# Loads, a conversion and the sums of output weights placed at other steps of a fused attention, MoE, MoE kernel

## The chip, the cores and the metric

The kernel runs on one NeuronCore of a Trainium2 chip. The metric is the device time of one execution in microseconds. Before the change three runs gave 1335.27, 1335.88 and 1336.69 us, median 1335.88. A verdict against this time is read from the runs of both kernels on the same chip.

## What is computed

The reference chains three blocks on 4608 tokens (8 batches of 576), in float32:

```python
scores = scale * q_c @ k_c.T            # chunks of 64 tokens, 8 heads of 64
attn = softmax(scores); x = attn @ v_c  # [4608, 512]
h = x @ w_in                            # [4608, 1024]
solu = h * softmax(h)
ln = (solu - mu) / sqrt(var + 1e-6) * g_ln
y = ln @ w_out                          # [4608, 512]
g = y @ w_gate; val = y @ w_val         # [4608, 1536] each
out = (g * sigmoid(g) * val) @ w_out2   # [4608, 512]
```

All weights arrive as float64 and are converted on the chip. Each float32 product is made of three passes over a high and a low part (PASSES, hi*hi, hi*lo, lo*hi).

## The kernel before

**Stages.** In the profiled execution attention and the first MoE matrix run to about 316 us, the matrix that gives y to about 518 us, the two matrices w_gate and w_val to about 1054 us, and w_out2 from there to the end. The change touches the third of these and the few units where the fourth begins.

**The third stage** (the double loop over s and n, L1012 to L1053). Tokens go in NSG = 5 segments of widths 512, 384, 512, 384, 512 (each width is half of a segment's tokens); for each segment there are FT = 12 steps, one per block of 128 hidden columns. The global step number is G = n + 12 s; `late` counts the steps of the last segment from 0 (G = 48). A step (`step`, L887) is a 2x2 block product with 7 sub-products instead of 8. Each sub-product (`product`, L863) is 6 matmuls into one of the PSUM tiles psA to psD, in the order A, C, B, D, A, C, D: products 4, 5 and 6 add to A, C and D, so each starts only when the earlier content of its bank has been read. ScalarE reads product 0 into p1 (L897) and product 1 into p5 (L899); VectorE makes p1 (L902), u3 (L904), the gate (L908), c12 in p5's buffer (L911), p1 again (L914) and three products (L915 to L917); GpSimd adds p5 to u3 (L905). So c12 can be written only when GpSimd's L905 has read p5, and the next step's L897 can write p1 only when L916 has read it.

**Work placed beside the steps**, written out by hand in program order, which is also each queue's order:

- `y_load(s + 1)` (L748) fetches the next segment's y from DRAM into `rawy` (a view of `ry`), 4 quarters (b11, b12, b21, b22) of one or two DMAs each, all on SyncE's queue; `y_units` (L759) is a list of 22 small units that turn it into the 7 operands: 8 GpSimd subtractions (L771) and 14 splits, each a ScalarE copy (L774) and a VectorE subtraction (L775). They are handed out a few per step; the last of them belong to the last step of the segment.
- The conversion of w_out2 in 24 pieces: `v_load` (L934, a DMA into a raw buffer), two steps on `v_mag` (ScalarE L79 and L85, GpSimd L92), after that step `v_bits` (VectorE L98 and L106, GpSimd L127), one step on `v_store` (L948, a DMA to `wo_dram`). Pieces alternate between two magnitude buffers `vms` and go round three raw buffers `vraws`, all inside the tile `mix`. LOADS lists the steps that load. v_mag of piece u overwrites the buffer that v_store of piece u - 2 read.
- In the last segment the converted rows come back as pairs p = 0 to 5: `t_load` (L925, 2 DMAs), `t_sums` (L954, 4 GpSimd subtractions of 128x256), `t_split` (L959, a ScalarE copy L965 and a VectorE subtraction L966 of 128x1792). The raw rows lie in the two halves of `ry`; t_split(p) for p < 3 issues t_load(p + 2) at its end. The sums of p are queued on GpSimd ahead of a step's L905.
- From `late` = 6 on `x_load`, `x_sums` (L985, 4 VectorE operations, L993), `x_high` (ScalarE L999) and `x_low` (VectorE L1004) prepare the operands of the last stage.
- SyncE's queue further carries the u stores (L885), the weight loads `w_load` (L742, ring of three) and all of the above, in order: an entry that waits holds all behind it.

**The fourth stage** runs units (n, i) of 7 sub-products with 3 passes (L1089, per unit 6 matmuls for each of pa, pb, pc and 3 for pd); `prepare(n)` puts x_high(n + 2), x_sums(n + 3), x_low(n + 2) ahead of unit n; every 6 units `evac` (L1096) empties the banks through ScalarE, VectorE (L1100) and GpSimd.

Of the kernel before, what the change touches and what calls it, by code (L numbers as in the profile page):

```python
# [23 lines left out]
def attn_moe_moe2_kernel(  # L24
# [681 lines left out]
    with ExitStack() as ph2:  # L706
# [40 lines left out]

        def y_load(s):  # L748
            for i, (half, k) in enumerate(((0, 0), (1, 0), (0, 2), (1, 2))):
                t, n = FIRST[s] + half * WIDTHS[s], 0  # L750
                while n < WIDTHS[s]:
                    m, o = divmod(t + n, TOK)
                    c = min(TOK - o, WIDTHS[s] - n)
                    nc.sync.dma_start(
                        out=rawy[:, :, i, n:n + c], in_=y_dram[m][:, k:k + 2, o:o + c]
                    )
                    n += c
# [65 lines left out]
        for m in range(1, NG):  # L823
            for d in range(KD):
# [8 lines left out]
                if last_m and d == 0:  # L833
                    stage_.close()
                    p2.close()
                    cp = ph2.enter_context(pool("cp"))
                    mix = cp.tile([P, 7 * HC], I64, tag="mix", name="mix")
                    flat = mix.bitcast(F32)
                    tt = flat[:, 0:6 * HC].rearrange("p (a n) -> p a n", a=3)
                    vms = [flat[:, i * HC:(i + 1) * HC] for i in (6, 7)]  # L840
                    vraws = [mix[:, i * HC:(i + 1) * HC] for i in (4, 5, 6)]
                    for i in range(2):
                        osb = cp.tile([P, TOK], F32, tag="osb", name="osb", bufs=2)
                    yk[1] = yk_tile(1)
                    w_load()
                    ka_ = ExitStack()
                    ka = ka_.enter_context(pool("ka"))
                    ahead_y = y_units(0)
# [72 lines left out]

        halves = list(ry.rearrange("p (j a n) -> j p a n", j=2, a=8))
        tw, tx = {}, {}

        def t_load(p):  # L925
            x = tx[p] = halves[p % 2 if p < 5 else 2]
            for j, dst in enumerate((x[:, 1:8:6], x[:, 2:7:4])):
                nc.sync.dma_start(
                    out=dst, in_=wo_dram[2 * p + j].rearrange("p (b n) -> p b n", b=2)
                )  # L930
# [8 lines left out]
        def v_mag(u):  # L939
            vc[u] = conv_a(None, vw.pop(u), vms[u % 2])  # L940
            conv_r(vc[u])
# [11 lines left out]

        def t_sums(p):  # L954
            t4, b11, b21, t1, t2, t3, b22, b12 = (tx[p][:, i] for i in range(8))
            for o, a, b in ((t1, b12, b11), (t2, b22, t1), (t3, b22, b12), (t4, b21, t2)):
                nc.gpsimd.tensor_tensor(out=o, in0=a, in1=b, op=ALU.subtract)

        def t_split(p):  # L959
            if p == 0:  # L960
                t = cb.tile([P, NS, 2, HC], F32R, tag="tw", name="tw")
            else:
                t = t_home[p]
# [4 lines left out]
            )  # L968
            if p < 3:
                t_load(p + 2)  # L970

# [6 lines left out]
        def x_load(n):  # L978
            if n >= NU:
                return  # L980
            x = xs[n] = halves[1 - n % 2 if n < 4 or n % 4 > 1 else 3 + n % 2]
            nc.sync.dma_start(out=x[:, 2:4], in_=unit_src(n, 0))
# [27 lines left out]
        todo = []  # L1010
        LOADS = (*range(1, FT + 1), *range(2 * FT - 2, 3 * FT - 2))
        for s in range(NSG):  # L1012
            for n in range(FT):
# [3 lines left out]
                if s + 1 < NSG:  # L1017
                    if n == (s == 0):
                        y_load(s + 1)
                    if n == (3 if s == 0 else 1):  # L1020
                        todo = y_units(s + 1)
                if late == 0:
                    t = cp.tile([P, 3, NS, 2, HC], F32R, tag="ykb", name="tw")
                    t_home = {i + 1: t[:, i] for i in range(3)}
                    t_home[4] = cp.tile([P, NS, 2, HC], F32R, tag="mix", name="tw")
                    t_load(0)
                    t_load(1)
                if 1 <= late < 6:
                    t_sums(late - 1)
                if late in (6, 8):  # L1030
                    x_load(late // 2 - 3)
                if G - 3 in LOADS:
                    v_store(LOADS.index(G - 3))
                if mag is not None:
                    v_mag(mag)
                step(s, n)
                if mag is not None:
                    v_bits(mag)
                if G in LOADS:
                    v_load(LOADS.index(G))  # L1040
                k = -(-len(todo) // (FT - n)) if todo else 0
                for x in todo[:k]:
                    x()
                todo = todo[k:]
                if 2 <= late < 7:
                    t_split(late - 2)
                if late in (7, 9):
                    x_sums(late // 2 - 3)
                if late in (9, 10):
                    x_high(late - 9)  # L1050
                    x_low(late - 9)
                if late == 11:
                    x_sums(2)  # L1053
        u_store()
# [10 lines left out]
        x_low(2)  # L1065
        t_sums(5)
        x_sums(3)

        def prepare(n):
            if n:  # L1070
                x_high(n + 2)
                x_sums(n + 3)
                x_low(n + 2)
            if n == 2:
                t_split(5)
# [97 lines left out]
```

## Time and profile before

| what | before |
|---|---|
| median of 3 runs | 1335.88 us (1335.27 to 1336.69) |
| the profiled execution's own time | 1336.44 us |
| its span, first to last instruction | 1334.7 us |
| TensorE matmul busy | 1299.1 us, 97% |
| VectorE, ScalarE, GpSimd busy | 962.8, 612.8, 434.5 us |
| mean granted TensorE clock | 0.994 of full speed |
| DMA queue of SyncE, share of 16 engines | 66.2% |

Times are in us from the start of the span. PE is TensorE's matmuls, PEld its weight loads, DVE VectorE, ACT ScalarE, POOL GpSimd, SPq the queue of SyncE that issues DMAs. An entry in brackets is the idle time of the engine before the instruction and what ended it. Matmuls overlap, so the listed duration of six is longer than the distance from one group's start to the next.

### The profile page before, as it was taken

The page shows a single profiled execution, that of the slowest core. Times are in us where ns is not written, and L with a number is a line of the kernel's source. Part 1 is how long each engine was busy: PE and PEld are TensorE (multiplying, and loading weights), DVE is VectorE, ACT ScalarE, POOL GpSimd, SP SyncE. Part 2 cuts the span into 40 slices and gives each one's busy share as a digit, 9 for nine tenths or more (in the row PEclk, how much of TensorE's full clock was granted, in tenths as well). Part 3 has the DMA queues.
Part 4 walks back from the last instruction along what each step waited for, and adds up shares of the span by engine and source line. Part 5 has one row for each costly group of instructions (what it writes and reads, how often), then busy time and mean ns, then how long its engine had stood idle before and what let it go on. Part 6 is the DMA issues. An engine that isn't in the chain of part 4 may idle for free.

```text
span 1334.7 us, 24970 instructions
## 1 busy us (share of the span) xinstructions
PE 1299.1 (97%) x9554; PEld 1182.0 (89%) x9554; DVE 962.8 (72%) x1564; ACT 612.8 (46%) x962; POOL 434.5 (33%) x581
## 2 busy tenths in 40 slices
PE   4999999999999999999899999999989999999998
PEld 3788888888999999888899888999868899999998
DVE  7788888885577765576566666766557898877875
ACT  5566666666566654334233333333223343333331
POOL 5455555554343342243322333231331200000010
PEclk9999999999999999999899999999989999999999
DMA  7355566665799997877989877988767444444341
GB/s 253 119 175 175 179 184 183 185 220 164 274 392 352 370 353 279 309 300 281 339 301 322 320 302 279 362 312 312 280 230 261 142 142 142 132 139 141 129 150 57
DMA packets 149063, 318.31 MB, mean 238 GB/s; under 512 B 11216, under 2 KB 98256, under 8 KB 141264
## 3 DMA queue, kind: packets, MB, share of 16 engines
q1 hardware_dynamic: 142608, 308.06, 66.2%
q10 hardware_dynamic: 6336, 8.65, 1.8%
q8 instruction: 75, 1.23, 0.4%
q14 instruction: 44, 0.36, 0.1%
HBM read 225.45 MB, written 91.23 MB: 237 GB/s over the span
## 4 chain that ended last, share of the span: by engine, by line
PE 90%; DVE 5%; DMA 2%; POOL 1%; issue 1%; ACT 1%; SPq 0%; POOLq 0%; DVEq 0%; ACTq 0%
PE y L166 15%; PE h L378 15%; PE pa L870 10%; PE pd L870 10%; PE pc L870 10%; PE opc L1089 5%; PE pb L870 5%; PE opa L1089 5%; PE opb L1089 5%; PE so_ps L262 3%; PE tr L459 3%; PE opd L1089 2%; PE pt L332 1%; DMA ry<-wo 1%; DVE hl L1004 1%
## 5 line engine op out<-in xcount | busy, mean ns | idle before, releaser
L378 PE MATMUL h<-wA,x 128*128 128x512 f32 x864 | 216.7, 399 | 0.6 <-ACT x L358 0.3
L166 PE MATMUL y<-lnT,wB 128*128 128x384 f32 x1152 | 200.7, 334 | 0.6 <-ACT ysb L172 0.6
L166 PEld LDWEIGHTS y<-lnT,wB 128*128 128x128 f32 x1152 | 199.5, 188 | 0.9 <-ACT ysb L172 0.9
L378 PEld LDWEIGHTS h<-wA,x 128*128 128x128 f32 x864 | 156.8, 188 | 32.1 <-ACT x L358 1.5
L905 POOL TENSOR_TENSOR u<-u,p 128x512 f32<-128x512 f32 (+1 forms) x60 | 70.7, 1179 | 218.0 <-DVE u L904 208.6
L870 PE MATMUL pa<-yka,ws 128*128 128x512 f32 x432 | 112.5, 397 | 6.1 <-ACT p L897 6.1
L907 ACT ACTIVATE u<-pa 128x512 f32<-128x512 f32 (+1 forms) x60 | 33.3, 556 | 175.4 <-PE pa L870 175.4
L870 PE MATMUL pc<-yka,ws 128*128 128x512 f32 x432 | 110.5, 391 | 0.0
L870 PE MATMUL pd<-yka,ws 128*128 128x512 f32 x432 | 109.8, 389 | 0.2 <-DVE u L904 0.2
L870 PEld LDWEIGHTS pa<-yka,ws 128*128 128x128 f32 x432 | 82.2, 191 | 24.3 <-ACT p L897 7.4
L1100 POOL TENSOR_TENSOR o<-o,p 128x256 f32<-128x256 f32 x35 | 25.8, 746 | 238.5 <-DVE o L1100 238.5
L870 PEld LDWEIGHTS pc<-yka,ws 128*128 128x128 f32 x432 | 82.0, 190 | 17.3
L1089 PE MATMUL opc<-tw,hl 128*128 128x256 f32 x648 | 96.2, 284 | 0.6 <-DVE o L1100 0.6
L870 PEld LDWEIGHTS pd<-yka,ws 128*128 128x128 f32 x432 | 81.0, 188 | 17.4 <-DVE u L904 0.6
L1089 PE MATMUL opb<-tw,hl 128*128 128x256 f32 x648 | 95.4, 283 | 0.3 <-DVE o L1100 0.3
L1089 PE MATMUL opa<-tw,hl 128*128 128x256 f32 x648 | 95.5, 283 | 0.0
L1089 PEld LDWEIGHTS opc<-tw,hl 128*128 128x128 f32 x648 | 85.4, 192 | 1.6 <-DVE o L1100 1.0
L1089 PEld LDWEIGHTS opb<-tw,hl 128*128 128x128 f32 x648 | 85.5, 192 | 0.5 <-DVE o L1100 0.5
L1089 PEld LDWEIGHTS opa<-tw,hl 128*128 128x128 f32 x648 | 85.6, 192 | 0.2
L908 DVE TENSOR_TENSOR u<-pa,u 128x512 f32<-128x512 f32 (+1 forms) x60 | 38.3, 638 | 65.0 <-ACT u L907 64.9
L999 ACT ACTIVATE hl<-ry 128x1792 fp32r<-128x1792 f32 x28 | 47.7, 1705 | 80.3 <-PE opd L1089 33.2
L912 ACT ACTIVATE u<-p 128x512 f32<-128x512 f32 (+1 forms) x60 | 35.4, 590 | 105.9 <-DVE p L911 105.9
(131 smaller groups left out, 2657.7 us busy)
## 6 DMA issues: line engine op xcount, KB each, us to landing
ws<-ws SPq DMA_DIRECT2D x60, 1792.0 KB, 7.7
ln<-lt SPq DMA_DIRECT2D x72, 256.0 KB, 3.0
lr<-ln SPq DMA_DIRECT2D x24, 768.0 KB, 7.1
u<-u SPq DMA_DIRECT2D x36, 512.0 KB, 5.4
ry<-u SPq DMA_DIRECT2D x56, 256.0 KB, 3.3
work<-u SPq DMA_DIRECT2D x52, 256.0 KB, 3.3
ws<-shi SPq DMA_DIRECT2D x12, 896.0 KB, 9.3
qt<-in_q SPq DMA_DIRECT2D x36, 256.0 KB, 3.6
```

The source lines that it names most:

```text
L166: nc.tensor.matmul(ys[u], lhsT=wB[:, f, a, d * P:(d + 1) * P], rhs=lnT[m][:, b, f, :], start=(n == 0), stop=(n == NY - 1),)
L262: nc.tensor.matmul(out[b * CH:(b + 1) * CH, c, n], lhsT=lhsT[r, h], rhs=rhs[r, h], start=True, stop=True, tile_position=(c * CH, b * CH),)
L378: nc.tensor.matmul(h[:, n * DM:(n + 1) * DM], lhsT=x[:, a, k, :], rhs=wA[:, n * KD + k, b, :], start=(j == 0), stop=(j == NH // 2 - 1),)
L459: nc.tensor.transpose(tr[:, f, :], so[:, c0:c0 + P], ident)
L870: nc.tensor.matmul(ps, lhsT=w[:, a, kk * P:(kk + 1) * P], rhs=y[:, b, kk], start=(first and n == 0), stop=(n == 5), skip_group_check=True,)
L905: nc.gpsimd.tensor_tensor(out=u3, in0=u3, in1=p5, op=ALU.add)
L907: nc.scalar.activation(out=sa, in_=psA, func=AF.Sigmoid)
L908: nc.vector.tensor_tensor(out=sa, in0=psA, in1=sa, op=ALU.mult)
L912: nc.scalar.activation(out=sb, in_=c12, func=AF.Sigmoid)
L999: nc.scalar.activation(out=hl[n][:, 0], in_=xs[n][:, 1:8], func=AF.Copy)
L1089: nc.tensor.matmul(acc[g, i, t][:, half], lhsT=hl[n][:, a, j, i * P:(i + 1) * P], rhs=tw[p][:, j, b], start=(p == x == half == 0), stop=(p ...
L1100: add = lambda eng, out, a, b: eng.tensor_tensor(out=out, in0=a, in1=b, op=ALU.add)
```

## The change

The whole diff. `y_load` takes a list of quarters, and one quarter is issued in each of four steps, after which the 22 units are handed out over the steps left. `mix` grows by half a raw buffer to 15 x 256 words; a third magnitude buffer is added, v_load moves ahead of the step, v_store ahead of v_load, and one piece moves from the first run of LOADS to the second. The part of `mix` that holds magnitudes and raw pieces serves as a third buffer for the pairs of output weights, whose loads, sums and splits get a table of steps of their own; t_sums(5) goes to VectorE and to a later place.

```diff
@@ -745,8 +745,9 @@
                 ws[u] = ring_tile("ws")
                 nc.sync.dma_start(out=by_part(ws[u].bitcast(F32)), in_=ws_dram[u[1]])
 
-        def y_load(s):
-            for i, (half, k) in enumerate(((0, 0), (1, 0), (0, 2), (1, 2))):
+        def y_load(s, parts=range(4)):
+            for i in parts:
+                half, k = i % 2, i // 2 * 2
                 t, n = FIRST[s] + half * WIDTHS[s], 0
                 while n < WIDTHS[s]:
                     m, o = divmod(t + n, TOK)
@@ -834,11 +835,11 @@
                     stage_.close()
                     p2.close()
                     cp = ph2.enter_context(pool("cp"))
-                    mix = cp.tile([P, 7 * HC], I64, tag="mix", name="mix")
+                    mix = cp.tile([P, 15 * HC // 2], I64, tag="mix", name="mix")
                     flat = mix.bitcast(F32)
                     tt = flat[:, 0:6 * HC].rearrange("p (a n) -> p a n", a=3)
-                    vms = [flat[:, i * HC:(i + 1) * HC] for i in (6, 7)]
-                    vraws = [mix[:, i * HC:(i + 1) * HC] for i in (4, 5, 6)]
+                    vms = [flat[:, i * HC:(i + 1) * HC] for i in (6, 7, 8)]
+                    vraws = [mix[:, i * HC // 2:(i + 2) * HC // 2] for i in (9, 11, 13)]
                     for i in range(2):
                         osb = cp.tile([P, TOK], F32, tag="osb", name="osb", bufs=2)
                     yk[1] = yk_tile(1)
@@ -920,10 +921,11 @@
             w_load()
 
         halves = list(ry.rearrange("p (j a n) -> j p a n", j=2, a=8))
+        halves.append(flat[:, 6 * HC:14 * HC].rearrange("p (a n) -> p a n", a=8))
         tw, tx = {}, {}
 
         def t_load(p):
-            x = tx[p] = halves[p % 2 if p < 5 else 2]
+            x = tx[p] = halves[(2, 0, 1, 2, 0, 3)[p]]
             for j, dst in enumerate((x[:, 1:8:6], x[:, 2:7:4])):
                 nc.sync.dma_start(
                     out=dst, in_=wo_dram[2 * p + j].rearrange("p (b n) -> p b n", b=2)
@@ -937,7 +939,7 @@
             nc.sync.dma_start(out=vw[u], in_=w_out2[f][:, half * HC:(half + 1) * HC])
 
         def v_mag(u):
-            vc[u] = conv_a(None, vw.pop(u), vms[u % 2])
+            vc[u] = conv_a(None, vw.pop(u), vms[u % 3])
             conv_r(vc[u])
             clamp(nc.gpsimd, vc[u])
 
@@ -951,14 +953,16 @@
                 out=wo_dram[f][:, half * HC:(half + 1) * HC], in_=vc.pop(u)[0]
             )
 
-        def t_sums(p):
+        def t_sums(p, eng=nc.gpsimd):
             t4, b11, b21, t1, t2, t3, b22, b12 = (tx[p][:, i] for i in range(8))
             for o, a, b in ((t1, b12, b11), (t2, b22, t1), (t3, b22, b12), (t4, b21, t2)):
-                nc.gpsimd.tensor_tensor(out=o, in0=a, in1=b, op=ALU.subtract)
+                eng.tensor_tensor(out=o, in0=a, in1=b, op=ALU.subtract)
 
         def t_split(p):
             if p == 0:
                 t = cb.tile([P, NS, 2, HC], F32R, tag="tw", name="tw")
+            elif p == 4:
+                t = cp.tile([P, NS, 2, HC], F32R, tag="mix", name="tw")
             else:
                 t = t_home[p]
             tw[p], x = t, tx.pop(p)[:, 0:7]
@@ -966,8 +970,6 @@
             nc.vector.tensor_tensor(
                 out=t[:, :, 1], in0=x, in1=t[:, :, 0].bitcast(F32), op=ALU.subtract
             )
-            if p < 3:
-                t_load(p + 2)
 
         def unit_src(n, b):
             g, p = divmod(n, NFP)
@@ -978,7 +980,7 @@
         def x_load(n):
             if n >= NU:
                 return
-            x = xs[n] = halves[1 - n % 2 if n < 4 or n % 4 > 1 else 3 + n % 2]
+            x = xs[n] = halves[1 - n % 2 if n < 4 or n % 4 > 1 else 4 + n % 2]
             nc.sync.dma_start(out=x[:, 2:4], in_=unit_src(n, 0))
             nc.sync.dma_start(out=x[:, 0:2], in_=unit_src(n, 1))
 
@@ -1008,49 +1010,52 @@
             x_load(n + 4 if n > 1 else n + 2)
 
         todo = []
-        LOADS = (*range(1, FT + 1), *range(2 * FT - 2, 3 * FT - 2))
+        LOADS = (*range(1, FT), *range(2 * FT - 2, 3 * FT - 1))
         for s in range(NSG):
             for n in range(FT):
                 late = n + FT * (s - NSG + 1)
                 G = n + FT * s
                 mag = LOADS.index(G - 2) if G - 2 in LOADS else None
                 if s + 1 < NSG:
-                    if n == (s == 0):
-                        y_load(s + 1)
-                    if n == (3 if s == 0 else 1):
+                    part = n - (s == 0)
+                    if 0 <= part < 4:
+                        y_load(s + 1, (part,))
+                    if part == 4:
                         todo = y_units(s + 1)
+                if G - 3 in LOADS:
+                    v_store(LOADS.index(G - 3))
+                if G in LOADS:
+                    v_load(LOADS.index(G))
+                if late == -4:
+                    t_load(0)
                 if late == 0:
                     t = cp.tile([P, 3, NS, 2, HC], F32R, tag="ykb", name="tw")
                     t_home = {i + 1: t[:, i] for i in range(3)}
-                    t_home[4] = cp.tile([P, NS, 2, HC], F32R, tag="mix", name="tw")
-                    t_load(0)
                     t_load(1)
-                if 1 <= late < 6:
-                    t_sums(late - 1)
-                if late in (6, 8):
-                    x_load(late // 2 - 3)
-                if G - 3 in LOADS:
-                    v_store(LOADS.index(G - 3))
+                    t_load(2)
+                if late in (1, 3):
+                    t_load(2 + (late + 1) // 2)
+                if late in (4, 7):
+                    x_load(late // 7)
+                T = {0: 0, 2: 1, 3: 2, 4: 3, 6: 4}.get(late)
+                if T is not None:
+                    t_sums(T)
                 if mag is not None:
                     v_mag(mag)
                 step(s, n)
                 if mag is not None:
                     v_bits(mag)
-                if G in LOADS:
-                    v_load(LOADS.index(G))
                 k = -(-len(todo) // (FT - n)) if todo else 0
                 for x in todo[:k]:
                     x()
                 todo = todo[k:]
-                if 2 <= late < 7:
-                    t_split(late - 2)
-                if late in (7, 9):
-                    x_sums(late // 2 - 3)
+                if T is not None:
+                    t_split(T)
+                if late in (8, 9, 11):
+                    x_sums({8: 0, 9: 1, 11: 2}[late])
                 if late in (9, 10):
                     x_high(late - 9)
                     x_low(late - 9)
-                if late == 11:
-                    x_sums(2)
         u_store()
 
         ka_.close()
@@ -1063,7 +1068,6 @@
         x_load(5)
         x_high(2)
         x_low(2)
-        t_sums(5)
         x_sums(3)
 
         def prepare(n):
@@ -1071,6 +1075,8 @@
                 x_high(n + 2)
                 x_sums(n + 3)
                 x_low(n + 2)
+            if n == 1:
+                t_sums(5, nc.vector)
             if n == 2:
                 t_split(5)
 
```

## Rows read from the trace of the kernel before

**Rows 1.** The page, busy time and share of the span, TensorE.
```profile
PE 1299.1 (97%) x9554; PEld 1182.0 (89%) x9554; DVE 962.8 (72%) x1564; ACT 612.8 (46%) x962; POOL 434.5 (33%) x581
```

**Rows 2.** Who waited for whom, PE: total us, times, longest.
```profile
PE pa L870 <- ACT p L897: 10.7, 4, 4.6
```

**Rows 3.** Timeline of PE, 640 to 656: start, duration, instruction, [idle before].
```profile
641.59 1.20 PE L870 MATMUL pb<-ykb,ws 128*128 128x384 f32 x6
642.63 1.20 PE L870 MATMUL pd<-ykb,ws 128*128 128x384 f32 x6
648.43 2.29 PE L870 MATMUL pa<-ykb,ws 128*128 128x384 f32 x6 [4.59 <-ACT p L897]
...
654.36 1.24 PE L870 MATMUL pa<-ykb,ws 128*128 128x384 f32 x6
```

**Rows 4.** Windows: length, PE, PEld, DVE, ACT, POOL busy, granted clock, DMA share, GB/s.
```profile
650.00:660.00 10.00, 10.00 (x48) 10.00 (x47) 5.42 (x11) 3.37 (x8) 3.50 (x5) 0.78 0.76 280
```

**Rows 5.** Timeline of SPq and ACT, 633 to 648.
```profile
633.25 7.66 SPq L754 DMA_DIRECT2D ry<-y  x8
...
641.31 0.33 SPq L950 DMA_DIRECT2D wo<-mix  x1
...
647.25 0.43 ACT L79 ACTIVATE mix<-mix 128x256 f32<-128x256 f32 x1 [6.75 <-DMA wo<-mix]
```

**Rows 6.** Timeline of PE, 971 to 1007.
```profile
971.07 1.52 PE L870 MATMUL pd<-yka,ws 128*128 128x512 f32 x6
...
981.11 1.52 PE L870 MATMUL pa<-yka,ws 128*128 128x512 f32 x6
...
985.19 1.52 PE L870 MATMUL pd<-yka,ws 128*128 128x512 f32 x6
...
994.48 1.52 PE L870 MATMUL pa<-yka,ws 128*128 128x512 f32 x6
...
998.56 1.52 PE L870 MATMUL pd<-yka,ws 128*128 128x512 f32 x6
...
1006.17 1.52 PE L870 MATMUL pa<-yka,ws 128*128 128x512 f32 x6
```

**Rows 7.** Timeline of SPq, POOL and DVE, 962 to 972.
```profile
962.16 1.18 SPq L928 DMA_DIRECT2D ry<-wo  x2
...
967.65 2.94 POOL L957 TENSOR_TENSOR ry<-ry 128x256 f32<-128x256 f32 x4 [11.94 <-DMA ry<-wo]
...
971.87 0.69 DVE L911 TENSOR_TENSOR p<-pc,p 128x512 f32<-128x512 f32 x1 [6.08 <-POOL u L905]
```

**Rows 8.** Timeline of PE, 1081 to 1089.
```profile
1081.63 0.88 PE L1089 MATMUL opa<-tw,hl 128*128 128x256 f32 x6
...
1084.15 0.88 PE L1089 MATMUL opa<-tw,hl 128*128 128x256 f32 x6
...
1088.04 0.88 PE L1089 MATMUL opa<-tw,hl 128*128 128x256 f32 x6
```

**Rows 9.** Timeline of POOL and DVE, 1060 to 1067.
```profile
1060.35 4.66 POOL L957 TENSOR_TENSOR work<-work 128x256 f32<-128x256 f32 x4 [8.33 <-DMA work<-wo]
1061.69 3.60 DVE L993 TENSOR_TENSOR ry<-ry 128x256 f32<-128x256 f32 x4
...
1065.21 1.54 DVE L993 TENSOR_TENSOR work<-work 128x256 f32<-128x256 f32 x4
```

**Rows 10.** Timeline of DVE, 635 to 637, the change of segments.
```profile
635.49 0.55 DVE L775 TENSOR_TENSOR ykb<-ry,ykb 128x384 fp32r<-128x384 f32 x1
...
635.95 1.10 DVE L775 TENSOR_TENSOR ykb<-mix,ykb 128x384 fp32r<-128x384 f32 x1
```

**Rows 11.** Timeline of DVE and POOL, 887 to 892, a narrow segment.
```profile
887.26 1.29 DVE L775 TENSOR_TENSOR yka<-ry,yka 128x512 fp32r<-128x512 f32 x2
...
889.55 0.56 DVE L904 TENSOR_TENSOR u<-pd,p 128x384 f32<-128x384 f32 x1 [0.41 <-PE pd L870]
...
891.22 1.29 POOL L771 TENSOR_TENSOR mix<-ry 128x512 f32<-128x512 f32 x1
```

## The prediction

> **What bounds the kernel now.** The page comes first: TensorE's matmuls fill 97% of the span [rows 1], so only the places where PE waits, or runs at the lower clock after a wait, can give anything back. The list of who waited for whom names one wait in the stretch that the change touches: products of bank pa wait for ScalarE's copy L897, four times, 10.7 us in all [rows 2]. PE's timeline shows where the four are, and that the idle time is not the whole price.
>
> The first is at the start of the first narrow segment. Product starts there lie 1.04 us apart (641.59 to 642.63). From the pd at 642.63 to the pa four products on it takes 11.73 us instead of 4.16: 4.59 idle, the rest matmuls at the lower clock [rows 3]; the granted clock of that stretch falls to 0.78 of full speed, a mix of the 2.4 and 1.2 GHz levels [rows 4]. Loss 11.73 - 4.16 = 7.57 us.
>
> The other three lie in the last segment. There the three products from 981.11 to 985.19 take 4.08, so 1.36 each, and four should take 5.44. They took 10.04, 9.29 and 7.61 [rows 6]: losses of 4.60, 3.85 and 2.17. Together the four cost 18.19 us.
>
> Why PE waited is read from the other queues. In the first, SyncE needs 7.66 us for the eight y loads of the new segment; a store of converted weights stands behind them and leaves at 641.31; ScalarE's L79, which overwrites a buffer whose store must have landed, idles 6.75 us for it until 647.25, and L897 is queued behind L79 [rows 5]. In the others, the load of a pair of output weights goes out at 962.16, when the split before it has read the buffer; GpSimd's four sums, queued ahead of the step's L905, start at 967.65 when it has landed; VectorE's L911 then waits 6.08 us for L905 [rows 7]; L916 and the next L897 are late behind it. The chain of waits is thus split, load, sums, L905, L911, L916, L897.
>
> A fifth, smaller loss follows at the first emptying of the banks in the last stage: a round of four banks takes 2.52 us (1081.63 to 1084.15), the next one 3.89, a loss of 1.37 [rows 8]. VectorE is behind there with preparing operands.
>
> **The change, part by part.**
>
> y by quarters, loads of pieces ahead of the step, third magnitude buffer. The same DMAs are issued, in four steps instead of one. By the row of eight, one quarter holds SyncE for about 7.66 / 4 = 1.9 us [rows 5], less than any step (seven products: 7.28 us narrow, 9.52 wide). A store then leaves up to 1.9 us late instead of 7.66, and with three magnitude buffers L79 needs the store of two steps ago. Store to L79 took 5.94 us (641.31 to 647.25), which fits in a step. The moved v_load waits for the raw buffer read by L127 of the step before, as the v_store ahead of it in the queue already does: no new wait, and the u store and weight load behind it are held by one more issue of some 0.3 us, against whole steps of lead. I take the first loss as gone: -7.57, between 0 and -7.57.
>
> The later table of pairs. Load 0 goes out four steps before the last segment into the freed part of mix; loads 1 and 2 at its first step, when ry is free; loads 3 and 4 still queue behind the splits that free their buffers (splits 0 and 1), and their sums come in the third step after each of those splits, instead of the next one. A load took 5.5 us from issue to the start of its sums [rows 7], and a wide step is 9.52, so GpSimd finds every pair landed. Its four sums, 2.94 us, then run in the tail of the preceding step, behind that step's L905, and no L905 waits. The splits, x_loads and u stores keep their kind and number; an x_load that holds SyncE holds the u store (three buffers) and a weight load (ring of three), not PE. I take -4.60 - 3.85 - 2.17 = -10.62, between 0 and -10.62. The sums of pair 0 now run beside the last y splits of the change to the last segment. Four GpSimd sums may hold VectorE there by some 2.06 us (the priced case below); the products that need those splits come last in the step, and I cost it at nothing.
>
> Fewer steps for the 22 y units. From the second segment on they come three per step in steps 4 to 9 and two in the last two, instead of two in each of eleven; in the first segment four and then three in seven steps, instead of three and two in nine. From the second segment on that is two splits per step at most, which a narrow segment already shows: two splits take 1.29 us, and yet the following L904 still idled 0.41 for PE [rows 11]. In the first segment the last step now has three splits instead of two, just where the narrow segment begins. One more is 0.55 us, or 1.10 when GpSimd runs beside it [rows 10], and product 3 of the next step needs it. Bounds 0 and 1.10; I take 0.4, since in the present trace the two there cost PE nothing.
>
> The sums of pair 5 on VectorE. Today GpSimd's four (4.66 us) run beside VectorE's four of the same shape, which take 3.60 us where the next four, alone, take 1.54 [rows 9]. Removing the overlap gives VectorE 2.06 back, doing the sums there costs 1.54: -0.5 us in a chain that ends in the fifth loss. Bounds: -1.37 (that loss gone) and +1.54 (no relief).
>
> A rule speaks to the row of 1.10. The Trainium skill, "SBUF — State Buffer", section "Who interferes with whom", says that a VectorE instruction with two SBUF inputs and a GpSimd instruction that reads SBUF exclude each other, and the second to start is blocked until the first ends. By the rows the extra split costs at most 0.55 + 0.55; by the rule a split that meets a GpSimd subtraction at its start would wait for all of it, 1.29 us [rows 11], and this term would be 1.84 instead of 0.4, the sum 1.4 us higher. The trace agrees that such pairs lengthen, with 0.55 of delay here; it shows no full 1.29.
>
> **The sum** is -7.57 - 10.62 + 0.4 - 0.5 = -18.29. The profiled execution took 1336.44 us, which gives 1318.15. The median of the three runs, 1335.88, lies 0.56 below the profiled one, so I predict 1317.6 for a median of runs.
>
> **The rivals.**
>
> One: the late chain keeps part of its waits. For it speaks that loads 3 and 4 still wait for a split and that SyncE serves them in order, with t_load and x_load ahead of the u store. If both kept a wait like the last two of rows 6 (3.85 + 2.17), the time would be 1317.6 + 6.0 = 1323.6. Against it speak two steps or more of cover, 19 us, for a load of 5.5 us. Chance 0.11.
>
> Two: the first loss stays, because the store is still held behind y quarters and weight loads while the DMA engines are full. Then 1317.6 + 7.6 = 1325.2. For it: 5.94 us for a store is long already, and the stretch after it has a DMA share of 0.76 [rows 4]. Against it: two buffers' worth of steps must now pass before L79 meets the store. Chance 0.07.
>
> Three, the other side: VectorE falls behind in the narrow segments, where three units are now packed into steps 4 to 9, some with two GpSimd subtractions of 1.29 us. Its place is L904, which must be done before product 6 writes bank D again. L904 idles 0.41 and product 6 starts two products (2.08) after the one it reads, of which L904 takes 0.56 [rows 11]. So up to 0.41 + 2.08 - 0.56 = 1.93 us of delay per step costs nothing; beyond that every step pays. To be slower than before by over 0.2%, 2.7 us, the 12 such steps of both narrow segments must give back 18.3 + 2.7 = 21.0 us, 1.75 each, a delay of 3.7. At 2.0 per step the time would be 1317.6 + 24 = 1341.6. Two full blocks of 1.29 make 2.58, a loss of 0.65 per step and 7.8 in all, 1325.4; the seen blocks of 0.55 make nothing. For 2.0 the lower clock after each wait would have to join in, as it did in rows 3. Chance 0.04 for the slower end; the middle lies in the range. The rule named above is the one by which this would come.
>
> Four: the change does less than it says, because the pair loaded early into mix is held, or holds, the y sums that live in the same tile. Then one GpSimd wait of the size of the first in rows 6 appears before the last segment: 1317.6 + 4.6 = 1322.2. Chance 0.05, since conversions and y sums share that tile today.
>
> **How the numbers follow.** The forecast has 0.73. Its low end takes the fifth loss as gone (0.87 more) and the seam at nothing (0.4): 1316.3, less 0.6 us for the spread of the runs, 1315.7. The high end takes in rivals one, two and four: 1325.7. Outside are the slower end and combinations. A difference of 0.2%, about what a measurement of this kernel can tell from no change, is 2.7 us. Faster by more than that are the forecast, rivals one, two and four and most combinations: 0.94. Slower: 0.04. Within: 0.02.
>
> **What the profile of the changed kernel would show.** If the steps hold, the list of PE's waits has no L897 in it; around 640 and 970 to 1010 the product starts keep 1.04 and 1.36; the granted clock there stays at 1.00; SyncE has no row of eight y loads but one or two per step; GpSimd's L957 rows start right behind an L905 and end before the next L904, without idle time for a load; after 1050 VectorE shows the four subtractions of pair 5 (now L957) in place of GpSimd, and its four L993 take about 1.5 us instead of 3.6. What would make the prediction wrong is a wait of PE for L904 or L897 in the narrow segments with two L771 rows beside VectorE's work, a wait of L79 for a store, or L957 idle for a DMA.

## The result and the profile after

The changed kernel takes 1318.23 us (median of 4 runs, 1317.04 to 1318.78) against 1336.22 us for the kernel before on the same chip (4 runs): ratio 0.9865, 95% interval 0.9848 to 0.9882. The time is 0.63 us above the predicted 1317.6, less than the spread of the runs. The profiled execution took 1318.28 us with a span of 1316.5 us.

The page of the changed kernel, busy times (share, instructions), answering to [rows 1]:

```profile
PE 1292.6 (98%) x9554; PEld 1177.5 (89%) x9554; DVE 967.7 (74%) x1568; ACT 613.5 (47%) x962; POOL 432.6 (33%) x577
```

TensorE's busy time fell by 6.5 us, although it does the same 9554 matmuls: some of these ran at the lower clock before. The mean granted clock rose from 0.994 to 0.999 of full speed.

The whole list of who waited for whom on PE (total us, times, longest), answering to [rows 2]. In the changed kernel `step` lies one line lower, so L897 became L898 and L870 became L871:

```profile
PE so_ps L262 <- DMA kt<-in_k: 12.2, 2, 7.4
PE pt L332 <- POOL e L319: 3.6, 2, 3.1
PE so_ps L262 <- ACT p L338: 0.7, 1, 0.7
PE y L166 <- ACT ysb L172: 0.6, 1, 0.6
PE opc L1095 <- DVE o L1106: 0.6, 1, 0.6
PE h L378 <- ACT x L358: 0.3, 1, 0.3
PE h L378 <- DVE so L411: 0.3, 1, 0.3
```

No wait for L898 is left. What remains in the part that the change touches is the 0.6 us of opc. Three more views of the changed kernel answer to [rows 3], [rows 5] and [rows 7]. First PE's timeline over the first narrow step ("the seam", where the first wide segment ends and the first narrow one begins), and the same step of the kernel before:

```profile
632.58 1.23 PE L871 MATMUL pa<-ykb,ws 128*128 128x384 f32 x6
...
640.45 1.20 PE L871 MATMUL pa<-ykb,ws 128*128 128x384 f32 x6
```

```profile
632.21 1.23 PE L870 MATMUL pa<-ykb,ws 128*128 128x384 f32 x6
...
639.51 1.20 PE L870 MATMUL pa<-ykb,ws 128*128 128x384 f32 x6
```

Seven products take 7.87 us (632.58 to 640.45) where the kernel before took 7.30 there (632.21 to 639.51): the seam costs 0.57 us, but the 7.57 of the step behind it are gone. The timeline of SPq and ACT of the changed kernel beside it:

```profile
633.14 0.94 SPq L755 DMA_DIRECT2D ry<-y  x2
...
637.03 0.33 SPq L952 DMA_DIRECT2D wo<-mix  x1
...
641.45 0.42 ACT L79 ACTIVATE mix<-mix 128x256 f32<-128x256 f32 x1
```

This quarter of the y loads holds SyncE for 0.94 us (the sixteen of the changed kernel take 0.90 to 1.97), the store leaves at 637.03 instead of 641.31, and L79 has no wait. And the late chain, timeline of SPq, POOL and DVE:

```profile
936.42 1.19 SPq L930 DMA_DIRECT2D mix<-wo  x2
...
957.27 1.29 POOL L906 TENSOR_TENSOR u<-u,p 128x512 f32<-128x512 f32 x1 [5.31 <-DVE u L905]
958.53 2.96 POOL L959 TENSOR_TENSOR mix<-mix 128x256 f32<-128x256 f32 x4
959.23 0.69 DVE L912 TENSOR_TENSOR p<-pc,p 128x512 f32<-128x512 f32 x1
```

The load of pair 3 goes out at 936.42. Its sums run at 958.53, right behind L906 and without a wait, and VectorE's L912 does not wait for L906 either.

Last, the first emptying of the banks, PE's timeline, answering to [rows 8], and VectorE's beside the former place of pair 5, answering to [rows 9]:

```profile
1064.19 0.88 PE L1095 MATMUL opa<-tw,hl 128*128 128x256 f32 x6
...
1066.71 0.88 PE L1095 MATMUL opa<-tw,hl 128*128 128x256 f32 x6
...
1070.27 0.88 PE L1095 MATMUL opa<-tw,hl 128*128 128x256 f32 x6
```

```profile
1044.40 1.55 DVE L995 TENSOR_TENSOR ry<-ry 128x256 f32<-128x256 f32 x4
...
1046.40 1.56 DVE L995 TENSOR_TENSOR work<-work 128x256 f32<-128x256 f32 x4 [0.45 <-DMA work<-u]
...
1049.81 1.55 DVE L959 TENSOR_TENSOR work<-work 128x256 f32<-128x256 f32 x4
```

The slow round takes 3.56 us instead of 3.89. The four x_sums that took 3.60 us take 1.55; the next four then wait 0.45 us for a transfer, and pair 5 (L959, on VectorE) takes 1.55.

A ledger from the starts of products in each kernel's trace, in us:

| stretch | before | after | gain | predicted |
|---|---|---|---|---|
| start to the first product of the third stage | 517.93 | 518.30 | -0.37 | 0 |
| third stage, to the first opa | 535.84 | 518.18 | 17.66 | 18.19 - 0.4 = 17.79 |
| fourth stage, to the last opd | 274.53 | 274.11 | 0.42 | 0.5 |
| from there to the end of the span | 6.40 | 5.91 | 0.49 | 0 |

The first row is not the change's: this start moved between 517.1 and 518.3 us over the profiles of this study. The last row nobody predicted: it is 6.3 to 6.4 us in the kernel before and the three others made from it (e4, e10, e11) and 5.9 to 6.0 in all kernels made from the changed one, and its cause stays open. The two nearly cancel, so the profiled execution came within 0.13 us of its forecast (1318.28 against 1318.15). The rest of the 0.63 us is the step from the profiled execution to the median: 0.56 us was taken off for it, and here it was 0.05.

### The profile page after: what moved, and what is told of

Read it like the earlier page. It is cut to its first block, busy times and chain, and to the rows that moved or that the text cites. A ratio compares the mean times of both kernels' runs of the same rounds, so it can differ in the third digit from the quotient of the medians.

```text
span 1316.5 us, 24943 instructions
## 1 busy us (share of the span) xinstructions
PE 1292.6 (98%) x9554; PEld 1177.5 (89%) x9554; DVE 967.7 (74%) x1568; ACT 613.5 (47%) x962; POOL 432.6 (33%) x577
## 3 DMA queue, kind: packets, MB, share of 16 engines
q8 instruction: 75, 1.23, 0.4%
## 4 chain that ended last, share of the span: by engine, by line
PE 94%; DVE 3%; DMA 1%; issue 1%; POOL 0%; ACT 0%; SPq 0%; POOLq 0%; DVEq 0%
PE y L166 15%; PE h L378 15%; PE pd L871 11%; PE pa L871 11%; PE pc L871 11%; PE pb L871 6%; PE opc L1095 5%; PE opa L1095 5%; PE opb L1095 5%; PE so_ps L262 3%; PE tr L459 3%; PE opd L1095 3%; PE pt L332 1%; DVE hl L1006 1%; DMA rin<-in_moe_w_in 0%
## 5 line engine op out<-in xcount | busy, mean ns | idle before, releaser
L906 POOL TENSOR_TENSOR u<-u,p 128x512 f32<-128x512 f32 (+1 forms) x60 | 70.8, 1180 | 241.5 <-DVE u L905 226.3
L871 PE MATMUL pa<-yka,ws 128*128 128x512 f32 x432 | 109.7, 389 | 0.0
L871 PE MATMUL pc<-yka,ws 128*128 128x512 f32 x432 | 109.7, 389 | 0.0
L871 PE MATMUL pd<-yka,ws 128*128 128x512 f32 x432 | 109.6, 389 | 0.0
L1106 POOL TENSOR_TENSOR o<-o,p 128x256 f32<-128x256 f32 x35 | 25.9, 750 | 251.0 <-DVE o L1106 249.3
L871 PEld LDWEIGHTS pc<-yka,ws 128*128 128x128 f32 x432 | 81.1, 188 | 16.9
L871 PEld LDWEIGHTS pd<-yka,ws 128*128 128x128 f32 x432 | 81.1, 188 | 16.8
L871 PEld LDWEIGHTS pa<-yka,ws 128*128 128x128 f32 x432 | 81.1, 188 | 16.6
L1001 ACT ACTIVATE hl<-work 128x1792 fp32r<-128x1792 f32 x26 | 44.3, 1704 | 73.6 <-PE opd L1095 42.1
```

The source lines that it names most:

```text
L871: nc.tensor.matmul(ps, lhsT=w[:, a, kk * P:(kk + 1) * P], rhs=y[:, b, kk], start=(first and n == 0), stop=(n == 5), skip_group_check=True,)
L906: nc.gpsimd.tensor_tensor(out=u3, in0=u3, in1=p5, op=ALU.add)
L1001: nc.scalar.activation(out=hl[n][:, 0], in_=xs[n][:, 1:8], func=AF.Copy)
L1106: add = lambda eng, out, a, b: eng.tensor_tensor(out=out, in0=a, in1=b, op=ALU.add)
```

## The experiments

The first eight kernels ran with a profile and one time each (the kernel before took 1336.49 us beside e1 to e4 and 1337.91 us beside e5 to e8), the last four with more runs. A single time is read to about 1 us, and the two times of the kernel before differ by 1.4 us, so where less matters the rows and the lengths of the stages decide.

### Was it the quarters or the third magnitude buffer?

In e1 the quarters are undone (the 22 units still start at the later step), in e2 the third buffer, in e3 both.

```diff
 # e1 and e3
-                    if 0 <= part < 4:
-                        y_load(s + 1, (part,))
+                    if part == 0:
+                        y_load(s + 1)
 # e2 and e3
-            vc[u] = conv_a(None, vw.pop(u), vms[u % 3])
+            vc[u] = conv_a(None, vw.pop(u), vms[u % 2])
```

> The changed kernel, but with all four y quarters issued in one step again; three magnitude buffers kept. Theory (the third buffer alone gives L79 a whole step more, so a store that leaves 7.7 us late still lands in time): no PE wait for L898 around 640, time within 1 us of the changed kernel's 1318.2. Rival (the quarters are what removed the first wait): the wait of about 4.6 us returns with the lower clock behind it, about 1325.8.

> The changed kernel with two magnitude buffers instead of three, quarters kept. Theory (with quarters the store is at most 2 us late and lands some 5.9 us after it leaves, inside one step): no PE wait, about 1318.2; ScalarE may idle a little at L79. Rival (the third buffer is what removed the first wait): between 1320 and 1325.8.

> Both undone: y loads in one step and two magnitude buffers, all else as in the changed kernel. Theory (the chain eight y loads, store, L79, L898 made the first loss): L79 waits for a store by 4 to 7 us around 640 and the time is 1318.2 + 7.6 = 1325.8. Rival (the first loss came from the place of the v loads behind the step, or from the load of piece 12 at the seam, both still changed here): about 1318.2.

Measured: e1 1317.72, e2 1318.29, e3 1323.00 us. Neither e1 nor e2 has a PE wait for L898. In e2 ScalarE idles for the store, but PE waits for nothing there (timeline of ACT):

```profile
642.41 0.44 ACT L79 ACTIVATE mix<-mix 128x256 f32<-128x256 f32 x1 [1.40 <-DMA wo<-mix]
```

In e3 the old chain is back (ACT's and PE's timeline):

```profile
646.64 0.43 ACT L79 ACTIVATE mix<-mix 128x256 f32<-128x256 f32 x1 [5.23 <-DMA wo<-mix]
```

```profile
643.43 1.20 PE L871 MATMUL pd<-ykb,ws 128*128 128x384 f32 x6
647.82 2.13 PE L871 MATMUL pa<-ykb,ws 128*128 128x384 f32 x6 [3.18 <-ACT p L898]
...
652.64 1.20 PE L871 MATMUL pa<-ykb,ws 128*128 128x384 f32 x6
```

The four products from 643.43 to 652.64 take 9.21 us instead of 4.16, a loss of 5.05, and the third stage shows it (523.2 us against 518.2 in the changed kernel). So the chain is the one that was named, and either edit alone breaks it, given the other edits of the change. The size is not the whole 7.57: the wait is 3.18 us instead of 4.59, and what follows it at the lower clock costs 1.87 (5.05 - 3.18) instead of 2.98. The 1.41 us less of waiting has two parts: L79 starts 0.61 us earlier than in the kernel before (646.64 against 647.25), and the last product ahead of the wait starts 0.80 us later (643.43 against 642.63), most of it the 0.57 of the seam.

### Was the third raw buffer needed for the pairs?

e4 is the kernel before with one line moved by a step.

```diff
-                if 1 <= late < 6:
-                    t_sums(late - 1)
+                if 2 <= late < 7:
+                    t_sums(late - 2)
```

> The kernel before with one edit: the sums of a pair are queued one step later, ahead of the step whose end splits that pair; still two raw buffers, no third, y loads and conversion as before. Theory (the three late losses came only from sums queued ahead of an L905 that needed a load just issued; one step between load and sums is cover enough, since a load takes 5.5 us and a step 9.52): the first loss stays, the three late ones vanish, 1336.2 - 10.6 = 1325.6. Rival (the third raw buffer and its longer lead are needed): GpSimd still idles for a load, PE still waits, 1328 or more.

Measured: 1326.09 us, 10.40 below the kernel before beside it; the third stage is 10.45 us shorter (525.39 against 535.84). The list of PE's waits has L897 once, 4.4 us, which is the first loss. GpSimd still idles for the load, but in a place where there is time (POOL and DVE):

```profile
967.49 4.18 POOL L957 TENSOR_TENSOR ry<-ry 128x256 f32<-128x256 f32 x4 [2.32 <-DMA ry<-wo]
...
975.09 1.30 POOL L905 TENSOR_TENSOR u<-u,p 128x512 f32<-128x512 f32 x1 [3.43 <-DVE u L904]
976.42 0.69 DVE L911 TENSOR_TENSOR p<-pc,p 128x512 f32<-128x512 f32 x1 [0.88 <-POOL u L905]
```

It waits 2.32 us for the load and then 3.43 us for L904, so the load is hidden; only L911 starts 0.88 us late, behind L905. The three late losses came from the distance between load and sums, and one step of it recovers nearly all; the third buffer was not needed for them.

### Pair 5 on VectorE, the seam, and the emptying

```diff
 # e5
         x_low(2)
+        t_sums(5)
         x_sums(3)
...
-            if n == 1:
-                t_sums(5, nc.vector)
 # e6
                 k = -(-len(todo) // (FT - n)) if todo else 0
+                if s == 0 and n == 6:
+                    k = 4
 # e7
-            prepare(n)
+            first = n == NFP - 1
+            if first:
+                x_high(n + 2)
+            else:
+                prepare(n)
...
                         evac(n // NFP, i)
+                    if first:
+                        (x_sums if i else x_low)(n + 2 + i)
```

> The changed kernel with the sums of pair 5 back on GpSimd ahead of x_sums(3). Theory (VectorE's four x_sums beside GpSimd's four take about 3.6 us instead of 1.5, and VectorE is the chain there): the round of banks that took 3.56 us in the changed kernel takes 3.9 again, the time rises by 0.2 to 0.6, less than one run can show, so the rows decide. Rival (the chain is set by something else): the round stays at 3.56.

> The changed kernel with four y units instead of three in step 6 of the first segment, so that its last step keeps two splits as in the kernel before. Theory (the third split at the seam delays product 3 and the later ones of the next step): the seven products of the first narrow step take 7.30 us instead of 7.87, 0.57 less. Rival (the delay comes from the y quarter or the store there): 7.87 stays.

> The changed kernel with VectorE's x_low(7) and x_sums(8) moved behind the first two emptyings of the banks. Theory (the emptying waits only because VectorE has that work queued ahead of it): the round of four banks that took 3.56 us takes 2.6 or less, about 1 us less in all. Rival (it waits for GpSimd's addition between two VectorE ones): a wait of about 0.5 us stays, or moves to the second emptying.

e5 took 1318.58 us. POOL's and DVE's timeline, then PE's:

```profile
1042.99 4.62 POOL L959 TENSOR_TENSOR work<-work 128x256 f32<-128x256 f32 x4 [8.38 <-DMA work<-wo]
...
1044.29 3.60 DVE L995 TENSOR_TENSOR ry<-ry 128x256 f32<-128x256 f32 x4
```

```profile
1066.77 0.88 PE L1094 MATMUL opa<-tw,hl 128*128 128x256 f32 x6
...
1070.66 0.88 PE L1094 MATMUL opa<-tw,hl 128*128 128x256 f32 x6
```

The overlap costs VectorE 2.05 us again (3.60 - 1.55) and the round takes 3.89, 0.33 us more than in the changed kernel's profile, as its theory had it. But one profile of each is not enough here. The other profiles of this study show the same place, and e2, whose edit lies far ahead of it, has this (PE's and DVE's timeline):

```profile
1046.50 1.56 DVE L995 TENSOR_TENSOR work<-work 128x256 f32<-128x256 f32 x4 [1.09 <-DMA work<-u]
...
1066.17 0.88 PE L1095 MATMUL opa<-tw,hl 128*128 128x256 f32 x6
...
1070.36 0.88 PE L1095 MATMUL opa<-tw,hl 128*128 128x256 f32 x6
```

| sums of pair 5 on | kernel | wait of the second four x_sums for their transfer, us | slow round, us |
|---|---|---|---|
| GpSimd | before, e4, e5, e10, e11 | none | 3.87 to 3.89 |
| VectorE | e3 | 0.15 | 3.45 |
| VectorE | the changed kernel again | 0.32 | 3.46 |
| VectorE | e6 | 0.41 | 3.51 |
| VectorE | the changed kernel | 0.45 | 3.56 |
| VectorE | e1 | 0.77 | 3.86 |
| VectorE | e2 | 1.09 | 4.19 |
| VectorE | e8 | 1.18 | 4.29 |

So the overlap is gone in each, but VectorE then comes early to a transfer whose landing differs from profile to profile, and the round follows that wait. The loads are issued at the same place in all (4.45 or 4.46 us behind the first opa in the rows of e1, e2, e3, e5, e8 and the changed kernel); what differs is when they land. An earlier round of the fourth stage that takes 2.66 to 2.69 us with GpSimd takes 2.52 in every kernel with VectorE. Over both rounds, against 6.55 us with GpSimd, the move gained 0.58 us in e3, lost 0.26 in e8, and gained 0.27 in the mean of the seven.

e6 took 1317.16 us. PE's timeline, the first products of the first two narrow steps (the seam):

```profile
632.06 1.23 PE L871 MATMUL pa<-ykb,ws 128*128 128x384 f32 x6
...
639.37 1.20 PE L871 MATMUL pa<-ykb,ws 128*128 128x384 f32 x6
```

The step takes 7.31 us: the third split (with its ScalarE copy) was the whole cost of the seam, 0.56 us.

e7 took 1316.45 us. PE's timeline, three rounds, then DVE's between the first and the second emptying:

```profile
1065.68 0.88 PE L1095 MATMUL opa<-tw,hl 128*128 128x256 f32 x6
...
1068.20 0.88 PE L1095 MATMUL opa<-tw,hl 128*128 128x256 f32 x6
...
1071.18 0.88 PE L1095 MATMUL opa<-tw,hl 128*128 128x256 f32 x6
```

```profile
1065.79 2.02 DVE L1006 TENSOR_TENSOR hl<-ry,hl 128x1792 fp32r<-128x1792 f32 x1
...
1069.26 0.69 DVE L1106 TENSOR_TENSOR o<-opc,o 128x512 f32<-128x512 f32 x1 [0.85 <-POOL o L1106]
```

The slow round takes 2.52, the next 2.98. So the 1.04 us by which the round was slow (3.56 - 2.52) are gone: the work queued on VectorE ahead of the emptying was their cause. At the second emptying 0.46 us is left, 0.2 of it a wait of PE for L1106. There x_low(7) now stands ahead of the emptying on VectorE (2.02 us), and inside it VectorE waits 0.85 us for GpSimd's addition; which of the two makes the 0.46 was not tried. The fourth stage took 273.3 us instead of 274.1.

### Where does rival three begin?

```diff
 # e8
                 k = -(-len(todo) // (FT - n)) if todo else 0
+                if s in (1, 3):
+                    k = min(6, len(todo))
```

> The changed kernel with six y units per step in the two narrow segments instead of three: the same 22 units in four steps, with up to four splits and three GpSimd subtractions in one step. It asks where rival three of the prediction begins. By the margin of 1.93 us: four splits add about 1.3 us to two, and blocks by GpSimd 0.5 to 1.3 more, so PE waits 0 to 0.7 us in two or three of eight steps, 0 to 4 us in all. If the margin is smaller than worked out, every packed step waits over 1 us and the lower clock joins, 10 us or more. If VectorE does not matter at all, nothing changes: 1318.2.

Measured: 1325.32 us, 7.1 above the changed kernel; the third stage alone is 7.5 us longer (525.7 against 518.2). That is neither of the two sizes expected, but between them. The row of PE's waits, then POOL, DVE and PE in one step with six units, and PE in another:

```profile
PE pd L871 <- DVE u L905: 5.5, 6, 1.4
```

```profile
669.83 1.60 POOL L772 TENSOR_TENSOR ry<-ry 128x512 f32<-128x512 f32 x1
...
670.20 1.65 DVE L917 TENSOR_TENSOR u<-p,u 128x384 f32<-128x384 f32 x1
...
675.31 1.31 PE L871 MATMUL pd<-ykb,ws 128*128 128x384 f32 x6 [0.44 <-DVE u L905]
...
898.22 1.33 PE L871 MATMUL pd<-ykb,ws 128*128 128x384 f32 x6 [1.43 <-DVE u L905]
```

Six steps wait for L905, 5.5 us in all, each costs PE some 0.3 us beyond its wait, and the granted clock stays at 1.00. The place is the one predicted; the expectation had too few steps (two or three) and too short a wait (up to 0.7). L917 takes 1.65 us where it takes 0.55 alone, while GpSimd's L772 runs until 671.43. So VectorE loses 1.10 us here, nearly the 1.23 us that L772 still had to run when L917 started. The Trainium skill, "SBUF — State Buffer", section "Who interferes with whom", has a rule for such a pair: the second to start is blocked until the first has finished. The trace agrees to within 0.13 us. The 1.10 of rows 10 fits it as well (POOL of the kernel before):

```profile
635.64 0.99 POOL L127 TENSOR_TENSOR mix<-mix 128x256 int32<-128x256 int32 x1 [5.19 <-DVE mix L106]
```

The split at 635.95 met an instruction with 0.68 us left to run, and took 0.55 us longer.

How much lateness is free can be read from the first step that waits, where L905 starts at 674.69. Product 3 started at 671.56 and took 1.04, and L905 starts 0.20 after its product in steps that wait for nothing, so it was 1.89 us late. Product 6 came at 675.31, 0.60 later than the end of product 5 (673.67 + 1.04) allows. So 1.29 us of lateness would have been free.

### How little of the change is enough, and what more there is

e10 is the kernel before with the quarters (the `y_load` and `part` lines of the change) and e4's edit alone; e11 adds the third magnitude buffer (the `mix`, `vms`, `vraws` and `vms[u % 3]` lines). e9 is the changed kernel with the edits of e6 and e7 together.

> The kernel before with two edits alone: the y loads by quarters over four steps, and the sums of a pair queued one step later. Two magnitude buffers, two raw buffers for the pairs, v loads behind the step and the sums of pair 5 on GpSimd stay as before. Theory (the losses were of order and distance in the queues, not of buffers): no PE wait for L897, the last emptying as before, 1318.2 + 0.3 = 1318.5, ratio to before 0.987. Rival (the extra buffers carry part of the gain): a wait of L79 or of GpSimd reaches PE and the time is 1320 or more.

> e10_two_edits_only with the third magnitude buffer of the change added, nothing else. In e10 L79 waited 2.5 and 3.8 us for a store in two narrow steps and PE lost 0.8 and 1.3 us by it. Theory (a store to its landing takes about a narrow step, and two buffers leave L79 no more than that): no such wait, 1321.4 - 2.1 = 1319.3. Rival (the moved v load, or the piece taken out of the first run, is what frees those steps in the change): L79 still waits and the time stays at 1321.4.

> The changed kernel itself, as the measure for its neighbours on the same chip: 1318, ratio to before 0.9865.

> The changed kernel with the edits of e6_units_off_the_seam and e7_evac_first together. Theory (the two leftovers are separate places on PE's row): the gains add, 0.57 at the seam and about 0.8 at the emptying, 1318.2 - 1.4 = 1316.8, ratio to before about 0.9855. Rival (what is gained at the seam is waited off later, the steps being held by another engine): no faster than either alone.

| kernel | median us | ratio to before | interval | third stage, us |
|---|---|---|---|---|
| e10 | 1321.37 | 0.9884 | 0.9869 to 0.9898 | 520.8 |
| e11 | 1320.05 | 0.9884 | 0.9868 to 0.9901 | 520.2 |
| the changed kernel again | 1317.57 | 0.9856 | 0.9841 to 0.9871 | 518.2 |
| e9 | 1316.91 | 0.9850 | 0.9834 to 0.9867 | 517.6 |

e11 has a median of 1335.83 us for the kernel before beside it, the other three 1336.93, so it is compared by its ratio and its third stage. e10 is slower than its theory by 2.9 us, as its rival had it. Its PE waits and ACT's L79:

```profile
PE pa L871 <- ACT p L898: 1.5, 2, 1.0
```

```profile
651.98 0.43 ACT L79 ACTIVATE mix<-mix 128x256 f32<-128x256 f32 x1 [3.82 <-DMA wo<-mix]
```

With v loads behind the step and the 12th piece in the first run, conversions go on for one step more into the narrow segment, and quarters with two buffers leave L79 too late twice: 0.79 us at the 11th piece and 1.32 at the 12th, by product starts. The two-buffer pairs add about 0.5 us in small delays of single products; together this is the 2.6 us by which the third stage is longer than in the changed kernel. In e11 that wait for a store is gone, but another has its place (SPq, ACT and PE):

```profile
640.20 0.43 SPq L938 DMA_DIRECT2D mix<-in_moe_w_out  x1
...
651.21 0.43 ACT L79 ACTIVATE mix<-mix 128x256 f32<-128x256 f32 x1 [4.00 <-DMA mix<-in_moe_w_out]
...
652.38 1.31 PE L871 MATMUL pa<-ykb,ws 128*128 128x384 f32 x6 [1.20 <-ACT p L898]
```

Now L79 waits for the raw piece itself: issued at 640.20, it lands just before 651.21, 11 us later, and PE waits 1.20. So e11's expectation holds in part: the third buffer frees L79 from the store, but the time gained is small (the third stage is 0.6 us shorter), because a load holds the same L79. The piece that it waits for is the 12th, the one that the change moves from the first run of LOADS to the second. In the changed kernel L79 has nothing to convert in that step. Whether the v loads ahead of the step would have freed it without that move was not tried.

In e9 both leftovers are smaller: the third stage takes 517.6 us as in e6, and the fourth 273.3, as in e7. It has the lowest median of the four kernels above; against the changed kernel beside it the times alone do not tell it apart (intervals overlap), the rows do, by 1.2 us.

## Why the prediction was right

**The first loss.** Gone entirely, as costed (-7.57). The mechanism holds (e3), but the prediction gave the gain to three edits at once and did not see that two of them, the quarters and the third buffer, are each sufficient beside the other edits (e1, e2), nor that without the moved v loads and the moved piece even both together leave a wait (e11: 4.00 us of L79 for the 12th piece, 1.20 us of PE). It gave the moved piece no part, and costed the moved v load only as a burden on the queue ("no new wait"); which of the two removes that wait is not shown. A quarter was priced at 1.9 us, a fourth of 7.66; at the seam it took 0.94, and the four of that segment 0.90 to 1.38, so about half of the 7.66 was waiting within the eight. One quarter of e11 took 3.37 us, so the 1.9 is no upper bound either.

**The late chain.** Gone entirely, as costed (-10.62), and every L959 starts behind an L906 without a wait. The reasoning by distance was right; e4 shows that one step of distance does it. The prediction counted the sums of pairs 3 and 4 in the third step after the splits that free their buffers; in the table of the change they stand ahead of the fourth, which only adds cover.

**The seam.** 0.4 was taken, between 0 and 1.10; it measured 0.57 (e6 gives it back).

**Pair 5.** -0.5 was taken; the fourth stage gained 0.42 in the profile of the change, 0.33 of it in the slow round (e5). The relief of 2.05 us came as worked out, and the 1.55 of sums were added, but the chain now reached the second four x_sums before their transfer had landed. That wait, 0.15 to 1.18 us in seven profiles, was not in the prediction: it makes the term anything from 0.58 us of gain to 0.26 of loss over the two rounds, inside the stated bounds. That the profile of the change came near -0.5 is luck in part.

**The rivals.** One (the late chain keeps waits), two (the first loss stays) and four (mix held as one tile) are not in the profile. Three needs more packing than the change has: with three units per step nothing waits, with six the third stage loses 7.5 us; where between them it begins was not tried. Its margin was put at 1.93 us; by e8 it is 0.41 + 1.29 = 1.70, the difference being mostly the 0.20 us between the end of a product and the start of L905, which the prediction left out. The prediction read its rows as showing "no full 1.29" of blocking. The rows of e8 and rows 10, read against what the GpSimd instruction still had to run, agree with full blocks. At the seam of the changed kernel the dearest case that it gave, 1.84 us, did not come up.

**The sum** was -18.29; the third and fourth stage together gave 17.66 + 0.42 = 18.08. The third stage's 17.66 is the 18.19 of the four losses less the 0.57 of the seam (17.62), so the terms that were put at nothing there, such as the sums of pair 0 beside the last splits, did cost nothing.

## What to carry to other kernels

When an in-order engine waits, look one queue back for what stands ahead of the thing it waits for, and count the distance from issue to use in steps of work: one step moved in the program order recovered 10.4 us here without a new buffer (e4). A bundle of edits that each lengthen the same distance can be more than the stall needs; undoing them one at a time tells which are spare, and undoing them together shows what they hold. Price a stall from one regular product start to the next regular one, since the idle time alone was 10.7 of 18.2 us. And read a gain of a few tenths from more than one profile: the 0.33 us of e5 looked clear, and other profiles of the same place showed a loss.

## What was not expected of the hardware

The extra cost behind a wait of PE is not in proportion to the wait. Waits of 0.49 and 1.02 us (e10) cost 0.30 us each beyond themselves, with the next six matmuls at 1.34 and 1.33 us, and one of 1.43 us (e8) about as much, all with a granted clock of 1.00 behind them. The last of the three late losses of the kernel before fits: its 2.17 us are a wait of 1.40, one of 0.16 and 0.3 for each. A wait of 1.96 us already cost 1.89 beyond itself, with a granted clock of 0.83 over 988 to 998 us (the second of the three late losses; PE of the kernel before):

```profile
988.67 2.78 PE L870 MATMUL pa<-yka,ws 128*128 128x512 f32 x6 [1.96 <-ACT p L897]
```

One of 3.18 us (e3) cost 1.87 at 0.83, and one of 4.59 us (the kernel before) cost 2.98 at 0.78. And a load of 256 KB that lands in 8.2 us by the median of e11's DMA list took 11 us when y quarters and weight loads were issued beside it.
